# Two value casts moved from GpSimd to VectorE, and batch 2's key-value products, numerators and block 2's first units rearranged, in a fused attention and gated feed-forward kernel

## The chip, the cores and the metric

The kernel runs on one core of one Trainium2 chip. The metric is the device time of one execution in microseconds (us). Five engines work side by side, each through its own queue of instructions in order: TensorE (PE: matrix products, with its weight loads shown as PEld), VectorE (DVE), ScalarE (ACT), GpSimd (POOL) and SyncE (SP, which here only issues transfers). Results of PE land in PSUM, which has eight banks in this kernel's one PSUM tile `ps`; everything else works from the on-chip memory SBUF.

## The reference

Eight batches of linear attention with position weights, followed by a gated feed-forward network over all 4608 tokens:

```python
# q, k, v: (8, 8, 576, 64) float32;  theta = pi/2 * pos / 576
phi(x) = concat(max(x, 0) * cos(theta), max(x, 0) * sin(theta))     # 64 -> 128 features
kv  = einsum('bhsf,bhsd->bhfd', phi(k), v);   z = sum_s phi(k)
num = einsum('bhsf,bhfd->bhsd', phi(q), kv)
den = einsum('bhsf,bhf->bhs', phi(q), z) + 1e-6
x   = (num / den), heads side by side, reshaped to (4608, 512)
out = (gelu(x @ w_gate) * (x @ w_val)) @ w_out                       # 512 -> 1536 -> 512
```

## The kernel before, in words

The attention is worked batch by batch (576 tokens each, eight batches), the feed-forward network block by block (512 tokens each, nine blocks). The code writes out by hand the order in which instructions are given to each engine; no scheduler reorders them. The stages of one batch are these:

- **Loads** (`load`, L77, issued at L80). q, k and v of a batch arrive as float32 in halves of 576 KB. Batch 0 and batches 3 and later are issued from SP's queue, batches 1 and 2 from POOL's queue, which also issues the weights (L94, L95, L98). Each staged tensor has two buffers.
- **Features** (`prep`, L151). Each of nine token groups `j` of q and k is multiplied by its cosine on VectorE (L161) and by its sine on ScalarE (L159), and written as bfloat16 into `qp` or `kp`. There is one `qp` and one `kp` buffer, so the next batch's features wait until the last batch's have been read.
- **The value cast** (`cast_v`, L177, instruction at L178). v is cast from float32 to bfloat16 into `vx`, next to a column of ones that makes the denominators. There are two `vx` buffers, for even and odd batches. Batches 0 and 3 to 7 are cast by VectorE, batches 1 and 2 by GpSimd (L451 and L559), as two instructions of 128x1152 elements a batch.
- **Key-value products** (`kv_unit`, L234). PE does 72 small products (L240) of `kp` and `vx` into banks 6 and 7, head pair by head pair, and ScalarE copies them to `kv_sb` (L249, two instructions).
- **Turning q** (`turn_q`, L190). From batch 2 on, two transposing transfers on SP (L192) turn `qp` into `qT`. Batches 0 and 1 are turned on PE (`turn_j`, L455).
- **Numerators** (`nm_unit`, L279). For each of five tiles of 128 tokens of a batch, PE does eight products of `qT` and `kv_sb` (L281), into two banks (6 and 7 unless `b0` names others), and VectorE makes the quotients (L292 denominator, L293 reciprocal, L294 product) into an `x_sb` tile, of which there are six.
- **Turning x** (`turn_x`, L345). A transposing transfer on SP (L348) puts each `x_sb` tile into its columns of the block's `xT`. For batches 0 and 1 most of this is done on PE (`turn_x_pe`, L352).

A block's feed-forward has twelve `gv_unit`s (L366): eight products of 128x512 (L375, four for the gate, four for the value), a Gelu on ScalarE (L383) and a product on VectorE into `hT` (L384). Units use banks 0 and 1 and banks 2 and 3 in turn, so a unit needs the VectorE product of the unit before the last to be done. A unit can be split into two halves of 256 columns; the first half needs only the first 256 columns of `xT`. The output product (`o_part`, L402, instruction L405) follows one block later, four of twelve accumulation steps after each unit; ScalarE copies the result (L414) and SP stores it (`flush`, L397; L395).

The main loop runs over the blocks n = 1 to 8 and over the units jt = 0 to 11 of each; in block n it also prepares batch b = n + 1. Batch 1 is handled before the loop in the list `order`, which mixes its turning of q, its key-value products, its numerators and the last output products of block 0. In the loop, `t_kv` is the unit after which the key-value products of batch b come, `t_nm` the unit from which its numerators come, one tile a unit; `t_q` and `t_k` place the features of the batch after. Block 1's loop also computes the last features of q(2), has SP turn q(2) after unit 2, and computes k(2)'s features after units 2 to 4 (`prep_third`). Block 2 covers the last 128 tokens of batch 1 and the first 384 of batch 2, so its second 256 columns are numerator tiles 1 and 2 of batch 2. Units 0 and 1 of blocks 1, 2 and 3 are done in halves: first half of unit 0, first half of unit 1, then the second halves.

Of the kernel before, what the change touches and what calls it, by code (L numbers as in the profile page):

```python
# [16 lines left out]
def kernel(  # L17
# [13 lines left out]
    nc = tc.nc  # L31
# [6 lines left out]
    JT = J // 128  # L38
# [3 lines left out]
    NT = 5  # L42
# [21 lines left out]
    def bank(i):  # L64
        return ps[:, i]

    def bank16(i):
        return ps[:, i].bitcast(BF16)
# [69 lines left out]
        for _ in range(n):  # L138
            nc.tensor.matmul(bank(to), lhsT=dummy[:, 0:128], rhs=dummy, start=True, stop=True)  # L139

    act_copy, dve_copy, pool_copy = nc.scalar.copy, nc.vector.tensor_copy, nc.gpsimd.tensor_copy


    phi = {}
# [32 lines left out]
    def cast_v(b, m0, m1, copy, j0=0, j1=R):  # L177
        copy(  # L178
            vx_tiles[b % 2][:, m0:m1, j0:j1, 0:D],
            staged["v", b][:, m0:m1, j0 * D:j1 * D].rearrange("p m (j d) -> p m j d", d=D),  # L180
        )
# [97 lines left out]
    def nm_unit(b, t, b0=6):  # L279
        for h in range(H):  # L280
            nc.tensor.matmul(  # L281
                bank(b0 + h // 4)[:, (h % 4) * (D + 1):(h % 4 + 1) * (D + 1)],
                lhsT=q_cols(b, t, h),
                rhs=kv_sb[b][:, h // 2, h % 2, :],
                start=True,
                stop=True,
            )
        nm = ps[:, b0:b0 + 2, 0:4 * (D + 1)].rearrange("p g (h d) -> p g h d", h=4)
        den = attn2.tile([128, 2, 4], FP32, name="den")
        rec = attn2.tile([128, 2, 4], FP32, name="rec")  # L290
        x = xsp.tile([128, 2, 4, D], BF16, name="x_sb")
        nc.vector.tensor_scalar_add(den, nm[:, :, :, D], EPS)  # L292
        nc.vector.reciprocal(rec, den)  # L293
        nc.vector.tensor_tensor(  # L294
            x,
            nm[:, :, :, 0:D],
            rec[:, :, :, None].to_broadcast([128, 2, 4, D]),
            op=ALU.mult,
        )
        xs[b, t] = x.rearrange("p g h d -> p (g h d)")  # L300
# [44 lines left out]
    def turn_x(b, t):  # L345
        x = xs.pop((b, t))
        for blk, c, o, m in pieces(b, t):
            nc.sync.dma_start_transpose(  # L348
                out=xT_block(blk)[:, :, c:c + m], in_=x[o:o + m, :]
            )  # L350
# [15 lines left out]
    def gv_unit(n, jt, c0=0, w=BLK):  # L366
        xt = xT[n]
        js = slice(jt * 128, (jt + 1) * 128)
        b0 = 2 * (turn[0] % 2)
        turn[0] += 1  # L370
        if n not in hT:
            hT[n] = ffn.tile([128, JT, BLK], BF16, name="hT")
        for g, wt in ((0, wg_sb), (1, wv_sb)):
            for ct in range(CT):
                nc.tensor.matmul(  # L375
                    bank(b0 + g)[:, 0:w],
                    lhsT=wt[:, ct, js],
                    rhs=xt[:, ct, c0:c0 + w],
                    start=(ct == 0),
                    stop=(ct == CT - 1),  # L380
                )
        gel = ffn.tile([128, BLK], FP32, name="gel")
        nc.scalar.activation(gel[:, 0:w], bank(b0)[:, 0:w], AF.Gelu)  # L383
        nc.vector.tensor_mul(  # L384
            hT[n][:, jt, c0:c0 + w], gel[:, 0:w], bank(b0 + 1)[:, 0:w]
        )
# [33 lines left out]
    HALF = BLK // 2  # L420
# [27 lines left out]
        for m in (0, 2):  # L448
            load(nc.gpsimd, name, 2, m, m + 2)
    for m in (0, 2):  # L450
        cast_v(1, m, m + 2, pool_copy)  # L451
    for m in (0, 2):
        load(nc.gpsimd, "v", 2, m, m + 2)

    def turn_j(b, m0, m1, js, to, copy):  # L455

        n = len(js)
        for m in range(m0, m1):
            turn_q_pe(b, m, js, bank16(to)[:, (m - m0) * n * 128:])
        copy(  # L460
            qt_tile(b)[:, :, m0:m1, js[0] * 64:(js[0] + n) * 64].rearrange(
                "f i m (j p) -> f m j i p", j=n
            ),
            bank16(to)[:, 0:(m1 - m0) * n * 128].rearrange(
                "f (m j i p) -> f m j i p", m=m1 - m0, j=n, i=2
            ),
        )
# [68 lines left out]
    for what, *a in order:  # L536
        if what == "o":
            o_part(a[0], range(a[1], a[1] + 4), banks0[a[0]], act_copy)
        if what == "q":
            turn_j(1, a[0], a[1], range(a[2], a[2] + 4), a[3], (dve_copy, act_copy)[a[3] % 2])  # L540
        if what == "q8":
            turn_j(1, 0, 4, (R - 1,), a[0], dve_copy)
        if what == "k":
            prep("k", 1, 0, range(R))
            prep("k", 1, 1, range(7), eng=nc.scalar)
            prep("k", 1, 1, range(7, R))
        if what == "q2":
            prep("q", 2, 1, range(*a), eng=nc.scalar)
            prep("q", 2, 0, range(*a))
        if what == "kv":  # L550
            kv_unit(1)
        if what == "nm":
            nm_unit(1, a[0], a[1])
        if what == "xt":
            turn_x_pe(1, a[0], a[1], act_copy)
    for m in (0, 2):
        load(nc.sync, "q", 3, m, m + 2)
    for m in (0, 2):
        cast_v(2, m, m + 2, pool_copy)  # L559


    def prep_third(name, b, i):
# [4 lines left out]
    def loads(b, names=("q", "k", "v")):  # L567
        for name in names:
            for m in (0, 2):
                load(nc.sync, name, b, m, m + 2)  # L570
# [12 lines left out]
    turn[0] = 1  # L583
    for n in range(1, NB):
        b = n + 1
        t_kv, t_nm, t_q, t_k = {1: (5, 8, 12, 12), 2: (5, 7, 7, 9), 3: (2, 5, 6, 9)}.get(
            n, (1, 2, 4, 8)
        )
        for jt in range(JT):
            if n > 3 or jt > 1:  # L590
                gv_unit(n, jt)
            else:
                for i in range(2):
                    gv_unit(n, i, jt * HALF, HALF)
                    if n == 1:
                        j = JA + 2 * jt + i
                        prep("q", b, 1, (j,), eng=nc.scalar)
                        prep("q", b, 0, (j,))
                        if jt == i == 0:
                            turn_x_pe(1, 3, 5, act_copy)  # L600
            if jt % 3 == 1:
                flush()
            if b < B:
                if n == 1 and jt == 2:
                    prep("q", b, 0, (R - 1,))
                    prep("q", b, 1, (R - 1,), eng=nc.scalar)
                    turn_q(b)
                    nm_unit(1, NT - 1)
                if n == 1 and jt == 3:
                    turn_x(1, NT - 1)  # L610

                late = -(-(BLK - 64 * b) // 128)
                nms = [(b, jt - t_nm)] if 0 <= jt - t_nm < (late if n == 1 else NT) else []
                if n == 2 and jt < 2:
                    nms.append((n, 3 + jt))
                i = jt - t_nm - 1
                if 0 <= i < late:
                    turn_x(b, i)
                    if n == 1 and i == late - 1:
                        loads(b + 1, ("k", "v"))  # L620
                for bt in nms:
                    nm_unit(*bt)
                if jt == t_kv:
                    kv_unit(b)
                i = jt - 2 if n <= 2 else -1
                if 0 <= i < 3:
                    prep_third("k", b, i)
                i = jt - (3 if n == 2 else 0)
                if n in (2, 3) and 0 <= i < 2:
                    cast_v(b, 2 * i, 2 * i + 2, dve_copy)  # L630
                i = jt - 9
                if n > 2 and 0 <= i < 2 and b + 1 < B:
                    cast_v(b + 1, 2 * i, 2 * i + 2, dve_copy)
                if (n, jt) in q3:
                    cosines, sines_ = q3[n, jt]
                    prep("q", 3, 1, sines_, eng=nc.scalar)
                    prep("q", 3, 0, cosines)
                if n > 1 and b + 1 < B:
                    if 0 <= jt - t_q < 3:
                        prep_third("q", b + 1, jt - t_q)  # L640
                    if 0 <= jt - t_k < 3:
                        prep_third("k", b + 1, jt - t_k)
                for c, t in nms:
                    if t == NT - 1:
                        if c + 1 < B:
                            turn_q(c + 1)
                        if c + 2 < B:
                            loads(c + 2)
                        for i in range(-(-(BLK - 64 * c) // 128), NT):
                            turn_x(c, i)  # L650
            if n > 1:
                o_part(
                    4 * (n - 1) + jt // 3,
                    range(4 * (jt % 3), 4 * (jt % 3) + 4),
                    4,
                    act_copy,
                )
# [47 lines left out]
```

## Time and profile before

| What | Value |
|---|---|
| median of 4 runs | 328.16 us |
| the four runs | 327.78, 329.58, 327.08, 328.54 us |
| the profiled execution | 327.78 us, of which the span from first to last instruction is 325.7 us |
| mean granted TensorE clock | 0.997 |
| busy time in the span: PE, DVE, ACT, POOL | 318.4, 167.9, 160.0, 28.3 us |
| L375, full units | 2 x 392 products, 2 x 100.6 us busy |
| L405 | 420 products, 105.8 us busy |
| L178 on DVE | 12 casts, mean 769 ns |
| L178 on POOL | 4 casts, mean 1562 ns |

A product of 512 columns is listed with a mean of 379 ns although the next one begins some 216 ns after it (eight of them take 1.73 us in the chain), since the products run in a pipeline. So "busy" sums can't be added up to the span; distances from start to start can. The profiled execution's time lies 2.1 us above its span.

### The profile page before, as it was taken

Reading aid. Unit: us, or ns where it says so; the run is one execution under the profiler, and the core shown is the slowest. Engines: PE = TensorE matmul, PEld = TensorE weight load, DVE = VectorE, ACT = ScalarE, POOL = GpSimd, SP = SyncE. Lnnn points to the kernel's source line nnn. Section 1 sums busy time; section 2 is a strip of 40 time slices with the busy share of each in tenths; the row PEclk is TensorE's granted clock in tenths of the full one; section 3 lists DMA queues with packets and bytes.
Section 4 is the critical chain, followed back from the end, with each engine's and each line's share of the span. In section 5 each row is a group of like instructions: output and inputs, shape, how many; then the busy total and the mean of one; then the engine's idle time right before and its main releaser. Section 6 shows DMA issues by size and latency. Waiting matters only on the chain.

```text
span 325.7 us, 6332 instructions
## 1 busy us (share of the span) xinstructions
PE 318.4 (98%) x2438; PEld 164.7 (51%) x2438; DVE 167.9 (52%) x406; ACT 160.0 (49%) x341; POOL 28.3 (9%) x43
## 2 busy tenths in 40 slices
PE   8899999999999999999999999999999999999995
PEld 3585556555554564545544545445544444444443
DVE  5863666748765961794485448544532222222211
ACT  8755767946455833574466336642222233222220
POOL 2855462000000000000000000000000000000000
PEclk9999999999999999999999999999999999999998
DMA  7999999982999989959978991764421111111124
GB/s 271 244 192 270 302 345 338 225 132 49 309 140 362 232 104 269 324 104 163 377 160 122 311 295 42 102 104 102 90 65 40 35 32 32 35 32 32 34 65 97
DMA packets 69102, 53.57 MB, mean 164 GB/s; under 512 B 45392, under 2 KB 54352, under 8 KB 69072
## 3 DMA queue, kind: packets, MB, share of 16 engines
q1 hardware_dynamic: 59264, 41.23, 54.5%
q0 software_dynamic: 9648, 11.80, 15.8%
q8 instruction: 19, 0.31, 0.4%
q10 hardware_dynamic: 160, 0.13, 0.1%
q14 instruction: 11, 0.09, 0.1%
HBM read 37.75 MB, written 9.44 MB: 145 GB/s over the span
## 4 chain that ended last, share of the span: by engine, by line
PE 89%; DMA 6%; DVE 1%; POOL 1%; SPq 0%; issue 0%; ACT 0%; DVEq 0%
PE ps L375 54%; PE ps L405 28%; PE ps L281 3%; DMA wv_sb<-in_moe_w_val_dram 2%; PE ps L240 2%; DMA qf<-in_q_dram 2%; DMA qT<-qp 2%; PE ps L666 1%; PE ps L203 1%; POOL wg_sb L94 1%; DVE qp L161 0%; PE ps L356 0%; DVE hT L384 0%; DVE kp L161 0%; SPq L80 0%
## 5 line engine op out<-in xcount | busy, mean ns | idle before, releaser
L384 DVE TENSOR_TENSOR hT<-gel,ps 128x512 bf16<-128x512 f32 (+2 forms) x120 | 75.8, 633 | 132.5 <-PE ps L375 128.6
L383 ACT ACTIVATE gel<-ps 128x512 f32<-128x512 f32 (+2 forms) x120 | 66.7, 556 | 110.1 <-PE ps L375 107.1
L375 PE MATMUL ps<-xT,wv_sb 128*128 128x512 bf16 (+2 forms) x480 | 113.0, 358 | 0.3 <-DMA wv_sb<-in_moe_w_val_dram 0.3
L375 PE MATMUL ps<-xT,wg_sb 128*128 128x512 bf16 (+2 forms) x480 | 112.9, 358 | 0.0
L405 PE MATMUL ps<-wo_sb,hT 128*128 128x512 bf16 x420 | 105.8, 379 | 0.0
L375 PEld LDWEIGHTS <-wv_sb 128*128 128x128 bf16 x480 | 46.3, 98 | 47.7 <-DMA wv_sb<-in_moe_w_val_dram 0.6
L375 PEld LDWEIGHTS <-wg_sb 128*128 128x128 bf16 x480 | 45.8, 98 | 45.8
L405 PEld LDWEIGHTS <-hT 128*128 128x128 bf16 x420 | 38.3, 98 | 39.8
L414 ACT COPY o_sb<-ps 128x512 f32<-128x512 f32 x34 | 19.9, 585 | 29.6 <-PE ps L405 29.6
L159 ACT ACTIVATE qp<-qf,sin_t 128x256 bf16<-128x256 f32 x71 | 31.8, 502 | 1.6 <-DMA qf<-in_q_dram 0.9
L159 ACT ACTIVATE kp<-kf,sin_t 128x256 bf16<-128x256 f32 (+1 forms) x75 | 30.4, 477 | 0.9 <-DMA kf<-in_k_dram 0.9
L294 DVE TENSOR_TENSOR x_sb<-ps,rec 128x512 bf16<-128x512 f32 x38 | 26.3, 692 | 1.5 <-DVE rec L293 0.2
L161 DVE TENSOR_SCALAR qp<-qf,cos_t 128x256 bf16<-128x256 f32 x71 | 21.6, 353 | 4.4 <-DMA qf<-in_q_dram 4.4
L281 PEld LDWEIGHTS <-qT 128*128 128x128 bf16 x304 | 14.6, 98 | 8.2 <-DMA qT<-qp 0.7
L161 DVE TENSOR_SCALAR kp<-kf,cos_t 128x256 bf16<-128x256 f32 x63 | 18.1, 348 | 0.0
L281 PE MATMUL ps<-kv_sb,qT 128*128 128x65 bf16 x304 | 16.1, 194 | 0.4 <-DMA qT<-qp 0.4
L139 PE MATMUL ps<-dummy 128*128 128x512 bf16 x30 | 9.9, 478 | 1.5 <-POOL dummy L113 1.5
L249 ACT CAST kv_sb<-ps 128x260 bf16<-128x260 f32 x14 | 4.6, 382 | 13.0 <-PE ps L240 13.0
L240 PEld LDWEIGHTS <-kp 64*128 64x128 bf16 x504 | 8.6, 95 | 3.1 <-issue 3.0
L178 DVE CAST vx<-vf 128x1152 bf16<-128x1152 f32 x12 | 9.2, 769 | 0.8 <-DMA vf<-in_v_dram 0.8
L240 PE MATMUL ps<-vx,kp 64*128 64x65 bf16 x504 | 9.5, 191 | 0.0
L293 DVE RECIPROCAL rec<-den 128x8 f32<-128x8 f32 x38 | 7.7, 203 | 1.3
(52 smaller groups left out, 91.4 us busy)
## 6 DMA issues: line engine op xcount, KB each, us to landing
out_dram<-o_sb SPq DMA_DIRECT2D x70, 128.0 KB, 2.5
kf<-in_k_dram SPq DMA_DIRECT2D x12, 576.0 KB, 6.5
vf<-in_v_dram SPq DMA_DIRECT2D x12, 576.0 KB, 8.6
qf<-in_q_dram SPq DMA_DIRECT2D x10, 576.0 KB, 5.1
qf<-in_q_dram POOLq DMA_DIRECT2D x4, 576.0 KB, 12.1
kf<-in_k_dram POOLq DMA_DIRECT2D x4, 576.0 KB, 12.8
vf<-in_v_dram POOLq DMA_DIRECT2D x4, 576.0 KB, 10.8
wg_sb<-in_moe_w_gate_dram POOLq DMA_DIRECT2D x6, 256.0 KB, 9.2
```

Of the source, the lines that this page charges most:

```text
L139: nc.tensor.matmul(bank(to), lhsT=dummy[:, 0:128], rhs=dummy, start=True, stop=True)
L159: nc.scalar.activation(o, i, AF.Relu, scale=tab[:, j:j + 1])
L161: (eng or nc.vector).tensor_scalar(o, i, 0.0, tab[:, j:j + 1], op0=ALU.max, op1=ALU.mult)
L178: copy(vx_tiles[b % 2][:, m0:m1, j0:j1, 0:D], staged["v", b][:, m0:m1, j0 * D:j1 * D].rearrange("p m (j d) -> p m j d", d=D),)
L240: nc.tensor.matmul(bank(6 + i)[:, m * (D + 1):(m + 1) * (D + 1)], lhsT=kp[rr, m, j, :], rhs=vx[rr, m, j, :], start=(j == 0), stop=(j == R ...
L281: nc.tensor.matmul(bank(b0 + h // 4)[:, (h % 4) * (D + 1):(h % 4 + 1) * (D + 1)], lhsT=q_cols(b, t, h), rhs=kv_sb[b][:, h // 2, h % 2, :], ...
L294: nc.vector.tensor_tensor(x, nm[:, :, :, 0:D], rec[:, :, :, None].to_broadcast([128, 2, 4, D]), op=ALU.mult,)
L375: nc.tensor.matmul(bank(b0 + g)[:, 0:w], lhsT=wt[:, ct, js], rhs=xt[:, ct, c0:c0 + w], start=(ct == 0), stop=(ct == CT - 1),)
L383: nc.scalar.activation(gel[:, 0:w], bank(b0)[:, 0:w], AF.Gelu)
L384: nc.vector.tensor_mul(hT[n][:, jt, c0:c0 + w], gel[:, 0:w], bank(b0 + 1)[:, 0:w])
L405: nc.tensor.matmul(bank(to), lhsT=hT[n][:, jt, tt * 128:(tt + 1) * 128], rhs=wo_sb[:, jt, :], start=(jt == 0), stop=(jt == JT - 1),)
L414: copy(o_sb, bank(to))
```

## The change

There are four edits. Batches 1 and 2 are no longer cast on GpSimd: v(1) is cast by VectorE after q(1)'s last group has been copied, in the list before the loop, and v(2) by VectorE as one instruction after unit 5 of block 1. In block 1, the key-value products of batch 2 come after unit 7 instead of unit 5, and the numerators of batch 2, with the turning of x, are written at the head of units 9, 10 and 11 instead of at the end of units 8, 9 and 10, into banks 6/7, 4/5 and 6/7. In block 2, units 0 to 3 are done in halves instead of units 0 and 1. And in block 2, k(3)'s features, v(3)'s casts and the key-value products of batch 3 come one unit later.

```diff
-    for m in (0, 2):
-        cast_v(1, m, m + 2, pool_copy)
     for m in (0, 2):
         load(nc.gpsimd, "v", 2, m, m + 2)
...
         if what == "q8":
             turn_j(1, 0, 4, (R - 1,), a[0], dve_copy)
+            for m in (0, 2):
+                cast_v(1, m, m + 2, dve_copy)
...
     for m in (0, 2):
         load(nc.sync, "q", 3, m, m + 2)
-    for m in (0, 2):
-        cast_v(2, m, m + 2, pool_copy)
...
-        t_kv, t_nm, t_q, t_k = {1: (5, 8, 12, 12), 2: (5, 7, 7, 9), 3: (2, 5, 6, 9)}.get(
+        t_kv, t_nm, t_q, t_k = {1: (7, 9, 12, 12), 2: (6, 7, 7, 9), 3: (2, 5, 6, 9)}.get(
             n, (1, 2, 4, 8)
         )
         for jt in range(JT):
-            if n > 3 or jt > 1:
+            if n == 1 and jt >= t_nm:
+                nm_unit(2, jt - t_nm, (6, 4, 6)[jt - t_nm])
+                turn_x(2, jt - t_nm)
+            heads = (0, 2, 4, 2)[n] if n < 4 else 0
+            if jt >= heads:
                 gv_unit(n, jt)
             else:
                 for i in range(2):
-                    gv_unit(n, i, jt * HALF, HALF)
+                    half, unit = divmod(2 * jt + i, heads)
+                    gv_unit(n, unit, half * HALF, HALF)
...
-                late = -(-(BLK - 64 * b) // 128)
-                nms = [(b, jt - t_nm)] if 0 <= jt - t_nm < (late if n == 1 else NT) else []
+                nms = [(b, jt - t_nm)] if n > 1 and 0 <= jt - t_nm < NT else []
                 if n == 2 and jt < 2:
                     nms.append((n, 3 + jt))
+
+                late = -(-(BLK - 64 * b) // 128)
                 i = jt - t_nm - 1
-                if 0 <= i < late:
+                if n > 1 and 0 <= i < late:
                     turn_x(b, i)
-                    if n == 1 and i == late - 1:
-                        loads(b + 1, ("k", "v"))
+                if n == 1 and jt == JT - 1:
+                    loads(3, ("k", "v"))
...
-                i = jt - 2 if n <= 2 else -1
+                i = jt - 1 - n if n <= 2 else -1
                 if 0 <= i < 3:
                     prep_third("k", b, i)
-                i = jt - (3 if n == 2 else 0)
+                i = 2 * (jt - 5) if n == 1 else jt - (4 if n == 2 else 0)
+                if n == 1 and i == 0:
+                    cast_v(b, 0, 4, dve_copy)
                 if n in (2, 3) and 0 <= i < 2:
                     cast_v(b, 2 * i, 2 * i + 2, dve_copy)
```

More of the change, by code (lines that the diff above doesn't have):

```diff
@@ L139, in dummies @@
             nc.tensor.matmul(bank(to), lhsT=dummy[:, 0:128], rhs=dummy, start=True, stop=True)
-    act_copy, dve_copy, pool_copy = nc.scalar.copy, nc.vector.tensor_copy, nc.gpsimd.tensor_copy
+    act_copy, dve_copy = nc.scalar.copy, nc.vector.tensor_copy
     phi = {}
```

## The prediction

> **What bounds the kernel now.** I read the page's busy table first (PE 318.4 us of a 325.7 us span, no other engine above 168), then the chain of waits, then each engine's timeline from 40 to 104 us, where all edits lie.
>
> In the chain, outside the start, one stretch is not PE:
>
> ```profile
> 64.84 1.03 PE L375 MATMUL ps<-xT,wg_sb 128*128 128x512 bf16 x4
> 65.71 1.03 PE L375 MATMUL ps<-xT,wv_sb 128*128 128x512 bf16 x4
> 66.67 1.51 PE L240 MATMUL ps<-vx,kp 64*128 64x65 bf16 x72
> ...
> 67.26 6.53 DMA qT<-qp
> ...
> 73.30 0.19 PE L281 MATMUL ps<-kv_sb,qT 128*128 128x65 bf16 x1
> 73.84 0.40 PE L281 MATMUL ps<-kv_sb,qT 128*128 128x65 bf16 x7 [0.35 <-DMA qT<-qp]
> 74.08 1.02 PE L375 MATMUL ps<-xT,wg_sb 128*128 128x512 bf16 x4
> ...
> 75.80 0.42 PE L281 MATMUL ps<-kv_sb,qT 128*128 128x65 bf16 x8
> 76.06 1.02 PE L375 MATMUL ps<-xT,wg_sb 128*128 128x512 bf16 x4
> 76.92 1.03 PE L375 MATMUL ps<-xT,wv_sb 128*128 128x512 bf16 x4
> 77.86 0.42 PE L281 MATMUL ps<-kv_sb,qT 128*128 128x65 bf16 x8
> ```
>
> (Start and length in us; the line at 67.26 is from the chain, the others from PE's timeline.) The starts matter, since products overlap. The first numerator tile of batch 2 reaches PE at 73.30, does one product and waits for the second transfer that turns q(2), which lands at 67.26 + 6.53 = 73.79. An undisturbed tile takes 0.26 us (75.80 to 76.06), this one 0.78: **0.52 us lost**. Next, four products take 0.86, so the third tile was due at 76.92 + 0.86 = 77.78; it starts at 77.86, just after the second tile's quotients end at 77.80: **0.08 lost**. Last, the key-value products were due at 66.57, begin at 66.67 and take 1.44 us, while the two neighbours take 1.26: **0.28 lost**, of which 0.1 is also seen ahead of the neighbours. Adding one start after another in this way from 40 to 104 us, I find only one other gap above 0.1 us (0.12 at 57.66, not touched). So everything that the edits could free is 0.52 + 0.28 + 0.08 = 0.88 us, 0.27% of the time. That cap governs what follows.
>
> **The change, part by part**, with the order in which both programs give instructions to each engine.
>
> *Numerators.* On PE they don't move. Before, tile 0 follows unit 8; at the head of unit 9 it still follows unit 8, and so for tiles 1 and 2. Ahead of tile 0 stand the same nine units, the key-value products and one tile of batch 1 in both. What sets the wait, the transfers that turn q(2), is gated by q(2)'s last cosine on VectorE (62.01) and SP's queue; SP's order of transfers is unchanged, and nothing ahead of 62 us is moved on VectorE but the cast of v(1) (below). So the landing stays at 73.79 and PE resumes at 74.08: 0. If the key-value products, two units later, run in 1.26, PE comes 0.28 us sooner and waits 0.28 longer: also 0. Banks 4/5 for tile 1 free tile 2 from the quotients just ahead: **−0.08**. On VectorE one cosine of q(3) (0.27 from start to start) now precedes each tile's quotients. Tile 0's cosine waits for the same landing, runs 73.8 to 74.1, and the quotients started at 74.28 anyway. Tiles 1 and 2 come 0.27 later, so `x_sb` of tile 2 is ready at about 80.05 instead of 79.78, and lands 2.4 us later (SP's x transfers there take 2.4 to 2.5), 82.5. Behind them SP issues k(3) and v(3), 0.27 later; k(3)'s first use is a unit later too.
>
> *Block 2's halves.* The second 256 columns were needed at 82.70 with tile 2 landing at 79.8 + 2.4 = 82.2, a margin of 0.5. Now four first halves come first, so they are needed one half-unit pair and one output step later, 2.6 to 2.9 us (82.70 to 85.57 before). The margin becomes some 3 us; as PE did not wait there in this execution, it is worth 0. The cost: four groups of four 256-column products take 1.75 (82.70 to 84.45), a full unit 1.73, so two more split units cost **+0.04** on PE. VectorE gets 2 x 0.42 for 0.69 and ScalarE 2 x 0.39 for 0.60, +0.15 and +0.2 a unit, while a unit with its output step lasts 2.59 on PE and both were idle for 1 to 2 us at these units (1.13 at 86.4 on VectorE, 2.04 on ScalarE).
>
> *v(1) on VectorE.* Two casts, by the DVE row:
>
> ```profile
> 46.66 0.42 DVE L460 COPY qT<-ps 128x512 bf16<-128x512 bf16 x1 [0.69 <-PE ps L203]
> 47.40 1.41 POOL L80 DMA_DIRECT2D vf<-in_v_dram  x2
> 48.28 1.33 PE L240 MATMUL ps<-vx,kp 64*128 64x65 bf16 x72
> ...
> 50.51 0.62 DVE L161 TENSOR_SCALAR qp<-qf,cos_t 128x256 bf16<-128x256 f32 x2 [3.43 <-DMA qf<-in_q_dram]
> ...
> 91.55 0.76 DVE L178 CAST vx<-vf 128x1152 bf16<-128x1152 f32 x1
> ...
> 43.57 3.89 POOL L178 CAST vx<-vf 128x1152 bf16<-128x1152 f32 x2 [2.98 <-DMA vf<-in_v_dram]
> 54.98 1.15 POOL L178 CAST vx<-vf 128x1152 bf16<-128x1152 f32 x1 [6.17 <-DMA vf<-in_v_dram]
> ```
>
> VectorE is free from 47.08 to 50.51, where it waits for q(2). 2 x 0.76 end at 47.84 and 48.60. PE wants the first at 48.28 and the second, half of the 72 products later, at 48.91: margins of 0.44 and 0.31, so 0 on the path; 1.52 of the 3.43 idle is used, and the next VectorE work still waits for q(2). Without that cover the 1.52 us would delay q(2)'s features and batch 1's quotients behind them.
>
> *v(2) on VectorE.* One cast of 128x2304, a shape that the trace doesn't show. Nearest row: 0.76 for half of it, so at most 1.52; the other end is POOL's slowest, 2.8 a half, 5.6. I take 1.5. It follows unit 5's product, which ends at 67.54, where VectorE idled 2.57 us; that idle was the key-value products' and moves, so unit 6's product, due at 68.35, starts at about 69.05, 0.7 late. Its banks are wanted by unit 8 at about 71.4: cover of 1.7 after it. The cast's own reader, the key-value products after unit 7, comes at about 70.0. 0.
>
> *POOL.* v(2)'s two loads no longer stand behind the casts. They are issued when their earlier transfers have landed, near 42 and 43.6 instead of 47.40 and 48.11. The loads of POOL's queue land in order, 1.4 to 1.5 us apart (issue plus landing time: q(2) 48.9 and 50.4, k(2) 51.9 and 53.4, v(2) 54.9 and 56.2), and the transfer engines are full from 30 to 58 us. So v(2) still lands near 55 to 56, and q(2) at 50.4: 0.
>
> The Trainium skill ("SBUF — State Buffer", section "SBUF: two separate sides") speaks against this edit: while VectorE runs certain copies and casts, GpSimd is locked out of a port and can't write the descriptors of its loads. By its example (620 ns become 3100) the two issues, now among VectorE's back-to-back cosines instead of in its idle stretch, would take 5 us more, an estimate; the sum would still not change, since the queue reaches them at 53.4. The rows show 0.70 to 0.75 us for POOL's issues throughout, beside busy VectorE or not. The page also says that a cast on GpSimd blocks VectorE; POOL's first cast did stretch to 2.8 us, but VectorE's cosines beside it kept 0.27 from start to start (nine in 2.44), so freeing VectorE from it is worth nothing by the row.
>
> *Batch 3's key-value products one unit later.* Same work. Numerator tile 0 of batch 3 follows two units later before and one unit later now; between them lie an output step and a unit (2.6 us) for the two copies to `kv_sb` (0.66): 0.
>
> **Sum.** −0.08 + 0.04 = −0.04 us: 327.7 on the profiled execution's own time (327.78). The median of the runs is 0.38 higher, so the same sum on it gives 328.1. I take **328.0**, nearer to the median, since a landing margin of 0.5 becomes 3, which can only help the runs above the profiled one. The runs spread from 327.08 to 329.58, so 0.5% (1.64 us) is about what a measurement of this kernel can tell from no change; the likeliest case's own range is 327.0 to 329.2.
>
> **Rivals.**
>
> *The casts of v(1) come too late (slower).* Place: 48.28 on PE. It begins to decide where one cast takes over 0.92 us (47.08 + 2 x 0.92 = 48.91). At POOL's undisturbed 1.15, 0.47 us is lost; at 2.8, the second ends at 52.68 and 3.77 is lost: 331.8 on the median. To pass 0.5% a cast would have to take 1.74 us. Against it: twelve VectorE casts of this shape have a mean of 0.769. For it: the margin is only 0.31, and all of it hangs on VectorE's in-order queue behind PE's last transposes. 6%.
>
> *v(2)'s early loads take bandwidth from q(2) (slower).* If all of v(2)'s 2 x 576 KB (3.0 us at 1.5 each) went ahead of q(2)'s second half, VectorE would wait until 53.4, and batch 1's first quotients, wanted at 52.66 with 0.5 to spare (their end at 52.16), would stop PE for 2.5: 330.7. It decides from 0.5 us of delay. Against it: in-order landings above. 6%.
>
> *The wait at 73.3 goes after all, or the unprofiled runs hold waits at block 2's start that the halves take away (faster).* All 0.88 less the 0.04 gives 327.3 on the median, still within 0.5%; a gain of 1.64 needs 0.8 us more that this trace doesn't show. The transfers that turn q(2) would have to land 0.5 sooner, for which nothing is moved. 8% beyond 0.5%; smaller gains belong to the no-change case.
>
> *The edit doesn't do what it says:* true of the numerators on PE, and in the sum.
>
> **How the numbers follow.** Forecast and its near neighbours, no change within 0.5%: 80%. Slower 12% (6 + 6), faster 8%. The range goes from 326.7 (all 0.88 gone from the profiled execution's 327.78, and 0.2 for the other runs' waits) to 329.6, which takes in the smaller stalls of both slower rivals (up to 1.4) and leaves their far ends out.
>
> **What will show it.** The first numerator tile of batch 2 still waits for the turned q(2) until about 73.8 to 74; tile 2 starts without a gap; VectorE's two casts lie between 47.1 and 48.7, with key-value products at 48.3; v(2) lands near 55 to 56; the second halves of block 2 begin at about 85.6 without a wait; PE's busy time is the same within 0.3 us. I am wrong if PE shows a new wait on `vx`, on q(2) or on `hT` of unit 6, or if the transfers that turn q(2) land at another time.

## The result, and the profile after

The changed kernel takes 326.83 us in the median of 43 runs (325.98 to 327.96). The kernel before takes 327.70 in 64 runs made beside them (326.50 to 329.78). The ratio of the means is 0.9965, with a 95% interval of 0.9955 to 0.9976: faster by 0.35%, well clear of no change, though inside the 0.5% that the forecast took as its bound.

More telling than the medians is how the runs are spread (counts of runs, rounded to quarters of a microsecond):

```
us       before  changed          us       before  changed
326.00             2              328.00             1
326.25             7              328.25     1
326.50     4       4              328.50     8
326.75     3      14              328.75     8
327.00     6       6              329.00     4
327.25    13       5              329.25     5
327.50     6       3              329.50     3
327.75     2       1              329.75     1
```

The kernel before has two groups of times: 34 runs at or under 328.0 with a mean of 327.14, and 30 above with a mean of 328.88. (It is not the clock: the three profiled executions of the upper group, below, had a mean granted clock of 0.999 to 1.000, and over the 122 runs of the kernel before that were made beside the experiments the mean is 0.9989 in the upper group and 0.9993 in the lower one, 0.04% apart where the times are 0.5% apart.) The changed kernel has no run above 328.0; its mean is 326.81. So of the 1.14 us between the two means (327.957 and 326.815), 30/64 x (328.88 − 327.14) = 0.82 is the upper group going, and 327.14 − 326.81 = 0.33, to rounding, is the rest. The profile of before that the prediction was read from is of the lower group.

The changed kernel's profiled execution (326.73 us, span 324.9) answers to the lines shown of before. These are PE's and VectorE's timelines: start, length, engine, line, operation, shapes and count, and in brackets an idle time before it with what ended it.

```profile
41.73 2.80 DVE L161 TENSOR_SCALAR kp<-kf,cos_t 128x256 bf16<-128x256 f32 x9
...
43.84 1.89 PE L405 MATMUL ps<-wo_sb,hT 128*128 128x512 bf16 x8
45.71 0.38 PE L203 MATMUL ps<-ident,qp 128*128 128x128 bf16 x4
...
46.47 1.42 DVE L178 CAST vx<-vf 128x1152 bf16<-128x1152 f32 x2
47.75 1.33 PE L240 MATMUL ps<-vx,kp 64*128 64x65 bf16 x72
...
66.93 1.36 DVE L178 CAST vx<-vf 128x2304 bf16<-128x2304 f32 x1
68.20 0.68 DVE L384 TENSOR_TENSOR hT<-gel,ps 128x512 bf16<-128x512 f32 x1
...
72.59 0.19 PE L281 MATMUL ps<-kv_sb,qT 128*128 128x65 bf16 x1
73.12 0.40 PE L281 MATMUL ps<-kv_sb,qT 128*128 128x65 bf16 x7 [0.33 <-DMA qT<-qp]
...
75.08 0.42 PE L281 MATMUL ps<-kv_sb,qT 128*128 128x65 bf16 x8
...
77.07 0.42 PE L281 MATMUL ps<-kv_sb,qT 128*128 128x65 bf16 x8
```

VectorE's casts of v(1) end at 47.89, and the key-value products, which need only the first of the two at their start, begin at 47.75 without a wait; the cast of v(2) takes 1.36 and makes unit 6's product start at 68.20, with no one waiting. Tile 0 of batch 2 still waits for the turned q(2), from 72.59 to 73.12. Tile 2 starts at 77.07, when it is due (0.08 gained). From q(1)'s first turning (40.13 before, 39.47 after) to the end of the span it is 285.57 us before and 285.43 after: 0.14 less. What lies ahead of that point is untouched by the edits and simply came 0.66 sooner. (In all 18 profiled executions, of whatever kernel, q(1)'s first turning follows the first value products of block 0's unit 2 by 19.54 to 19.56 us. Those products start anywhere from 19.45 to 21.25; in the profile of before they wait 0.33 us for a weight load.) Inside their spans, then, the two profiled executions show next to nothing of a gain that 107 runs show clearly: most of it is in executions that were not profiled. Outside the spans there is a difference of 0.25 us, 327.78 − 325.7 = 2.08 before and 326.73 − 324.9 = 1.83 after; more on it at the end of the part on why the prediction was right or wrong.

### The profile page after: what moved, and what is told of

It is laid out like the page before. It is cut to its first block, busy times and chain, and to the rows that moved or that the text cites. A ratio compares the mean times of both kernels' runs of the same rounds, so it can differ in the third digit from the quotient of the medians.

```text
span 324.9 us, 6360 instructions
## 1 busy us (share of the span) xinstructions
PE 318.4 (98%) x2454; PEld 166.5 (51%) x2454; DVE 170.4 (52%) x411; ACT 160.0 (49%) x343; POOL 22.1 (7%) x39
## 4 chain that ended last, share of the span: by engine, by line
PE 90%; DMA 5%; ACT 2%; DVE 1%; SPq 1%; issue 0%; DVEq 0%; ACTq 0%
PE ps L375 54%; PE ps L405 28%; PE ps L281 3%; DMA qf<-in_q_dram 3%; PE ps L240 2%; DMA qT<-qp 2%; ACT kp L159 1%; PE ps L671 1%; SPq L80 1%; PE ps L203 1%; PE ps L356 1%; ACT gel L383 0%; DVE qp L161 0%; DVE x_sb L321 0%; SPq L192 0%
## 5 line engine op out<-in xcount | busy, mean ns | idle before, releaser
L375 PEld LDWEIGHTS <-wv_sb 128*128 128x128 bf16 x488 | 47.3, 98 | 46.4
L375 PEld LDWEIGHTS <-wg_sb 128*128 128x128 bf16 x488 | 46.6, 98 | 45.4
L178 DVE CAST vx<-vf 128x1152 bf16<-128x1152 f32 (+1 forms) x15 | 12.0, 806 | 0.8 <-DMA vf<-in_v_dram 0.8
```

Source lines behind the costliest of these rows:

```text
L178: copy(vx_tiles[b % 2][:, m0:m1, j0:j1, 0:D], staged["v", b][:, m0:m1, j0 * D:j1 * D].rearrange("p m (j d) -> p m j d", d=D),)
L375: nc.tensor.matmul(bank(b0 + g)[:, 0:w], lhsT=wt[:, ct, js], rhs=xt[:, ct, c0:c0 + w], start=(ct == 0), stop=(ct == CT - 1),)
```

## The experiments

Each was run beside the kernel before on the same chip (35 runs of it beside the first three sets each, 17 beside the fourth). "Over 328.0" counts the runs above the gap between the two groups.

### First set: one part alone, or one part undone

**e1, the halves alone.** Block 2's first four units in halves, put into the kernel before:

```diff
-            if n > 3 or jt > 1:
+            heads = (0, 2, 4, 2)[n] if n < 4 else 0
+            if jt >= heads:
...
-                    gv_unit(n, i, jt * HALF, HALF)
+                    half, unit = divmod(2 * jt + i, heads)
+                    gv_unit(n, unit, half * HALF, HALF)
```

> The kernel before with block 2's first four units in halves and nothing else. The times of the kernel before lie in two groups, about 326.5 to 327.8 us and 328.2 to 329.8 us (28 of 64 in the upper one); those of the changed kernel lie between 326.0 and 328.0. Theory X (late x): in the upper group the turned x of batch 2's tiles 1 or 2 lands after the second 256 columns of block 2 are due at 82.70, where the profiled execution had 0.45 us to spare, and PE waits some 1.5 us. Then this kernel has no upper group: all times under about 328.0, median 327.0 to 327.3, ratio near 0.997. Theory C (casts): the upper group comes from GpSimd's cast of v(1), which took 2.8 us where others took 1.15, being late for the key-value products. Then the upper group stays, ratio within 0.999 to 1.001. Theory K (batch 3): it comes from k(3) landing late for its features after units 2 to 4 of block 2; then the upper group stays too.

Ratio 1.0006 (0.9981 to 1.0031), 7 of 12 runs over 328.0. The upper group stays; theory X falls.

**e2, the changed kernel without the two additional halved units.**

```diff
-            heads = (0, 2, 4, 2)[n] if n < 4 else 0
+            heads = (0, 2, 2, 2)[n] if n < 4 else 0
```

> The changed kernel with only units 0 and 1 of block 2 in halves, as before; all else changed. Theory X: an upper group of times returns, some 1.5 us above the lower one, in nearly half of the executions; median 327.2 to 328.5, ratio 0.998 to 1.000. Theories C and K: no upper group, median about 326.8 as the changed kernel.

Ratio 0.9970 (0.9954 to 0.9987), 0 of 12 over 328.0, median 326.47. The halves are not needed for the gain.

**e3, the changed kernel with GpSimd's casts.** Both casts are put back to POOL's queue, all else stays changed (the line that defines `pool_copy` is left out here):

```diff
+    for m in (0, 2):
+        cast_v(1, m, m + 2, pool_copy)
     for m in (0, 2):
         load(nc.gpsimd, "v", 2, m, m + 2)
...
-            for m in (0, 2):
-                cast_v(1, m, m + 2, dve_copy)
...
+    for m in (0, 2):
+        cast_v(2, m, m + 2, pool_copy)
...
-                if n == 1 and i == 0:
-                    cast_v(b, 0, 4, dve_copy)
```

> The changed kernel with v(1) and v(2) cast by GpSimd as before, all else changed. Theory C: the upper group returns, ratio 0.998 to 1.000. Theories X and K: as the changed kernel, about 326.8, ratio 0.996 to 0.997; the casts are worth nothing.

Ratio 0.9996 (0.9975 to 1.0018), 3 of 12 over 328.0: the upper group is back, and no gain is left that can be told from none. So the casts make it. But the place that theory C named was wrong: this run's profile fell in the upper group (328.89 us), and GpSimd's casts were quick there:

```profile
42.02 4.28 DVE L161 TENSOR_SCALAR kp<-kf,cos_t 128x256 bf16<-128x256 f32 x9
46.22 0.81 DVE L161 TENSOR_SCALAR kp<-kf,sin_t 128x256 bf16<-128x256 f32 x2
46.96 0.68 DVE L460 COPY qT<-ps 128x1024 bf16<-128x1024 bf16 x1
...
42.67 1.22 POOL L178 CAST vx<-vf 128x1152 bf16<-128x1152 f32 x1 [2.97 <-DMA vf<-in_v_dram]
44.13 1.18 POOL L178 CAST vx<-vf 128x1152 bf16<-128x1152 f32 x1 [0.23 <-DMA vf<-in_v_dram]
...
44.13 1.89 PE L405 MATMUL ps<-wo_sb,hT 128*128 128x512 bf16 x8
47.69 0.38 PE L203 MATMUL ps<-ident,qp 128*128 128x128 bf16 x4 [1.67 <-DVE qT L460]
```

The same rows in the profile of before:

```profile
42.39 2.44 DVE L161 TENSOR_SCALAR kp<-kf,cos_t 128x256 bf16<-128x256 f32 x9
45.28 0.69 DVE L460 COPY qT<-ps 128x1024 bf16<-128x1024 bf16 x1
...
44.51 1.89 PE L405 MATMUL ps<-wo_sb,hT 128*128 128x512 bf16 x8
46.23 0.39 PE L203 MATMUL ps<-ident,qp 128*128 128x128 bf16 x4
```

In e3 the casts took 1.2 us each, and VectorE's nine cosines beside them 4.28 instead of 2.44. Behind the cosines in VectorE's queue stands the copy that empties bank 2, and PE turns q(1)'s last group in that bank: it was due at 44.13 + 1.73 = 45.86 and began at 47.69. That gave theory P (port): GpSimd and VectorE block each other, now one and now the other; if VectorE loses, PE loses 1.8 us.

**e4, block 1's rearrangement alone**, with GpSimd's casts and the old block 2:

```diff
-        t_kv, t_nm, t_q, t_k = {1: (5, 8, 12, 12), 2: (5, 7, 7, 9), 3: (2, 5, 6, 9)}.get(
+        t_kv, t_nm, t_q, t_k = {1: (7, 9, 12, 12), 2: (5, 7, 7, 9), 3: (2, 5, 6, 9)}.get(
...
+            if n == 1 and jt >= t_nm:
+                nm_unit(2, jt - t_nm, (6, 4, 6)[jt - t_nm])
+                turn_x(2, jt - t_nm)
...
```

> The kernel before with block 1's rearrangement alone: batch 2's key-value products after unit 7, its numerators written at the head of units 9 to 11, banks 4/5 for tile 1. Theory X: two groups of times as before, both about 0.1 us lower by the banks; ratio 0.999 to 1.000. If the numerators' place matters after all (x earlier by more than the 0.08 us), the upper group shrinks or goes. Theory C and K: two groups, too.

Ratio 1.0000 (0.9977 to 1.0022), 3 of 12 over 328.0: two groups, nothing gained that can be measured. The 0.08 of the banks is too small for it.

### Second set: which cast, and by which way

**f1, only v(1) to VectorE** (the two lines of e3 for v(1), the other way round, in the kernel before).

> The kernel before with only v(1)'s two casts moved to VectorE (v(2) stays on GpSimd). Theory P (port): in the upper group of times GpSimd's casts of v(1) get ahead of VectorE's nine cosines of k(1), which then take 4.28 us instead of 2.44, the copy of turned q behind them comes 1.7 us late, and PE waits for its bank before q(1)'s last group. Then this edit alone removes the upper group: all times under 328.0, ratio 0.995 to 0.998, cosines 2.4 to 2.8 us in the trace. Rival R: the upper group needs both casts or comes from v(2)'s: then two groups stay, ratio 0.999 to 1.001.

Ratio 0.9978 (0.9958 to 0.9998), 0 of 12 over 328.0, median 326.78, cosines 2.58 in the profile. This one edit takes the upper group away.

**f2, only v(2) to VectorE**, ahead of the key-value products where they stood before:

```diff
-    for m in (0, 2):
-        cast_v(2, m, m + 2, pool_copy)
...
+                if n == 1 and jt == 4:
+                    cast_v(b, 0, 4, dve_copy)
```

> The kernel before with only v(2)'s cast moved to VectorE, as one instruction after unit 4 of block 1, ahead of the key-value products after unit 5 (v(1) stays on GpSimd). Theory P: two groups of times as in the kernel before, ratio 0.999 to 1.002. Rival R: no upper group, ratio 0.995 to 0.998.

Ratio 1.0048 (1.0019 to 1.0076). Two groups stay, 8 runs from 327.6 to 328.6 and 4 from 330.5 to 331.1, as theory P says, but 1.3 and 1.9 us higher than the two groups of before beside it, which neither theory expected. PE's timeline shows why:

```profile
64.58 1.03 PE L375 MATMUL ps<-xT,wv_sb 128*128 128x512 bf16 x4
67.15 1.34 PE L240 MATMUL ps<-vx,kp 64*128 64x65 bf16 x72 [1.54 <-DVE vx L178]
```

VectorE reaches the cast only after k(2)'s last cosines, and the key-value products after unit 5 wait for it. This is the work that the changed kernel's other move covers: with the cast on VectorE, the products must come later, and after unit 7 they do not wait.

**f3, one number:** q(1)'s last group turned in bank 6, both casts left on GpSimd.

```diff
-        + [("q8", 2), ("o", 1, 4), ("o", 2, 4), ("kv",), ("q2", 0, 2), ("o", 3, 4)]
+        + [("q8", 6), ("o", 1, 4), ("o", 2, 4), ("kv",), ("q2", 0, 2), ("o", 3, 4)]
```

> The kernel before with one number changed: q(1)'s last group is turned in bank 6 instead of bank 2, so PE doesn't wait for VectorE's copy of bank 2 ahead of it; both casts stay on GpSimd. Theory P: VectorE's cosines are stretched as often as before, but PE has no wait there beyond some 0.2 to 0.4 us at the key-value products: the upper group of times goes or shrinks to under 328.2, ratio 0.996 to 0.999. If the loss runs by another way (features of k(1) late, or GpSimd's loads of v(2) late), two groups stay, ratio 0.999 to 1.001.

Ratio 0.9977 (0.9957 to 0.9996), 0 of 12 over 328.0, highest 327.52. PE no longer needs the copy of bank 2 at that point, and the upper group is gone with the casts where they were. The edit acts first at PE's turning in bank 6, at 45.94 in this run's profile, when the first cast has begun (42.99) and the cosines have ended (44.54), so it is not how they meet that it changes. So the loss runs by that bank; that it runs by no other way is what the times say, since no trace caught stretched cosines with bank 6 (h3, below).

**f4, the numerators really one unit later** on PE, in the changed kernel:

```diff
-        t_kv, t_nm, t_q, t_k = {1: (7, 9, 12, 12), 2: (6, 7, 7, 9), 3: (2, 5, 6, 9)}.get(
+        t_kv, t_nm, t_q, t_k = {1: (7, 10, 12, 12), 2: (6, 7, 7, 9), 3: (2, 5, 6, 9)}.get(
...
                 if n == 1 and jt == JT - 1:
+                    nm_unit(2, 2, 6)
+                    turn_x(2, 2)
                     loads(3, ("k", "v"))
```

> The changed kernel with batch 2's numerators really one unit later on PE: tile 0 behind unit 9, tile 1 behind unit 10, tile 2 behind unit 11 of block 1. Both traces have PE wait 0.5 us at tile 0 for the turned q(2), landing near 73.1 to 73.8. If that wait is the next thing to go, PE reaches tile 0 at about 74.3, after the landing, and the time falls by 0.5 us against the changed kernel, to about 326.3, ratio 0.994 to 0.996. If x for block 2 then comes late (tile 0 is due at about 78.6 and would land at about 78.2), PE waits there instead and the time stays at 326.8, ratio 0.996 to 0.997.

Ratio 1.0031 (1.0011 to 1.0051), a loss that neither line expected. Timelines of ScalarE, VectorE, SP and PE:

```profile
75.04 0.91 ACT L159 ACTIVATE qp<-qf,sin_t 128x256 bf16<-128x256 f32 x2 [1.71 <-DMA qT<-qp]
75.13 0.42 PE L281 MATMUL ps<-kv_sb,qT 128*128 128x65 bf16 x8
...
76.46 0.69 DVE L384 TENSOR_TENSOR hT<-gel,ps 128x512 bf16<-128x512 f32 x1 [1.05 <-ACT gel L383]
...
77.33 0.16 DVE L292 TENSOR_SCALAR den<-ps 128x8 f32<-128x8 f32 x1
...
78.48 3.08 SPq L348 DMA_TRANSPOSE xT<-x_sb  x2
...
79.09 0.42 PE L281 MATMUL ps<-kv_sb,qT 128*128 128x65 bf16 x8
81.03 0.60 PE L375 MATMUL ps<-xT,wg_sb 128*128 128x256 bf16 x4 [1.51 <-DMA xT<-x_sb]
```

PE's wait for the turned q is gone (no bracket at 75.13), but ScalarE now waits 1.71 us for the same landing with q(3)'s sines, ahead of unit 9's Gelu; VectorE waits for that Gelu, and tile 0's quotients stand behind it: PE had finished tile 0 at about 75.4, its quotients begin at 77.33, its x is turned from 78.48, and block 2, due at 79.35, starts at 81.03. The 0.5 us wait was exchanged for one of 1.7 (79.35 to 81.03).

### Third set: the changed kernel again, and what is left at bank 2

**g1** is the changed kernel again, **g2** f1's and f3's edits together, **g3** the changed kernel with q(1)'s last group in bank 6, and **g4** the kernel before against itself. The edits are those shown.

> The changed kernel once more, beside the next three on one chip. Theory P: one group of times, median 326.4 to 326.9, ratio 0.995 to 0.998; in the trace PE waits 0.1 to 0.2 us at q(1)'s last group, since GpSimd's two issues of v(2)'s loads still take 0.3 us from VectorE's cosines (2.7 to 2.8 us for the nine).

Ratio 0.9971 (0.9949 to 0.9992), median 326.58, 0 of 12 over 328.0. The small wait was not there this time, since the collision went the other way. In POOL's and VectorE's timelines of g1

```profile
41.27 0.70 POOL L80 DMA_DIRECT2D vf<-in_v_dram  x1 [1.70 <-DMA wo_sb<-in_moe_w_out_dram]
42.76 2.51 POOL L80 DMA_DIRECT2D vf<-in_v_dram  x1 [0.79 <-DMA vf<-in_v_dram]
...
42.16 2.44 DVE L161 TENSOR_SCALAR kp<-kf,cos_t 128x256 bf16<-128x256 f32 x9
46.42 0.42 DVE L458 COPY qT<-ps 128x512 bf16<-128x512 bf16 x1 [0.69 <-PE ps L203]
```

the cosines are undisturbed, and the issue of v(2)'s second load takes 2.51 us where others take 0.72. In the first profile of the changed kernel the issues took 0.70 and 0.72 and the cosines 2.80.

> The kernel before with v(1) cast by VectorE and q(1)'s last group turned in bank 6; nothing else. If both edits only guard against the same loss, this is as either alone, ratio 0.996 to 0.998, one group of times. If the casts on VectorE, now behind the copy of bank 6, come late for the key-value products, 0.2 to 0.5 us are lost, ratio 0.997 to 0.999.

Ratio 0.9971 (0.9947 to 0.9994), 0 of 12 over 328.0: as either edit alone, so the two guard against the same loss.

> The changed kernel with q(1)'s last group turned in bank 6. Theory P: the 0.1 to 0.2 us that PE still waits there go: median 0.1 to 0.2 us under the changed kernel's, ratio 0.994 to 0.998. If nothing is left there: as the changed kernel.

Ratio 0.9961 (0.9941 to 0.9981), median 326.54 against g1's 326.58: the lowest ratio of all, but not to be told from the changed kernel.

> The kernel before once more, against itself. Two groups of times, ratio 1.000 within its interval. Where the profiled execution is of the upper group (about 4 in 10), theory P expects VectorE's nine cosines of k(1) at 4.0 us or more instead of 2.44, GpSimd's two casts of v(1) at about 2.4 us in sum instead of 3.9, and a wait of PE of 1.5 to 1.8 us for the copy of turned q ahead of q(1)'s last group; in the lower group none of these.

Ratio 0.9989 (0.9965 to 1.0013), 4 of 12 over 328.0. The profile was of the lower group: cosines 2.44, GpSimd's two casts 3.91 in sum, q(1)'s last group at 46.13 as due.

### Fourth set: the kernel before in its upper group

**h1 and h2** are one profiled execution each of the kernel before, **h3** is one of f3's kernel; **h4** casts v(1) on GpSimd in four instructions:

```diff
-    for m in (0, 2):
-        cast_v(1, m, m + 2, pool_copy)
+    for m in range(4):
+        cast_v(1, m, m + 1, pool_copy)
```

> The kernel before, one look. If the time is over 328.2: nine cosines of k(1) at 4.0 us or more, GpSimd's two casts of v(1) at about 2.4 us in sum, PE waits 1.5 to 1.8 us ahead of q(1)'s last group. If under 327.8: cosines 2.44, casts about 3.9 in sum, no wait. Anything else speaks against theory P.

> As the look before: one of the two pictures, and the one that its time calls for.

Both took 329.13 us, and both show the picture foretold. VectorE's, GpSimd's and PE's timelines of h1:

```profile
42.31 4.29 DVE L161 TENSOR_SCALAR kp<-kf,cos_t 128x256 bf16<-128x256 f32 x9
46.52 0.81 DVE L161 TENSOR_SCALAR kp<-kf,sin_t 128x256 bf16<-128x256 f32 x2
47.25 0.67 DVE L460 COPY qT<-ps 128x1024 bf16<-128x1024 bf16 x1
...
43.22 1.23 POOL L178 CAST vx<-vf 128x1152 bf16<-128x1152 f32 x1 [2.96 <-DMA vf<-in_v_dram]
44.66 1.20 POOL L178 CAST vx<-vf 128x1152 bf16<-128x1152 f32 x1 [0.21 <-DMA vf<-in_v_dram]
...
44.42 1.89 PE L405 MATMUL ps<-wo_sb,hT 128*128 128x512 bf16 x8
47.98 0.38 PE L203 MATMUL ps<-ident,qp 128*128 128x128 bf16 x4 [1.67 <-DVE qT L460]
```

and the same rows of g4, the lower group of the same code:

```profile
42.29 2.44 DVE L161 TENSOR_SCALAR kp<-kf,cos_t 128x256 bf16<-128x256 f32 x9
44.66 0.61 DVE L161 TENSOR_SCALAR kp<-kf,sin_t 128x256 bf16<-128x256 f32 x2
45.18 0.68 DVE L460 COPY qT<-ps 128x1024 bf16<-128x1024 bf16 x1
...
43.45 3.91 POOL L178 CAST vx<-vf 128x1152 bf16<-128x1152 f32 x2 [2.97 <-DMA vf<-in_v_dram]
...
44.40 1.89 PE L405 MATMUL ps<-wo_sb,hT 128*128 128x512 bf16 x8
46.13 0.39 PE L203 MATMUL ps<-ident,qp 128*128 128x128 bf16 x4
```

Read the pair down the columns: cosines 4.29 against 2.44, the copy of bank 2 at 47.25 against 45.18, q(1)'s last group 3.56 us behind the products ahead of it against 1.73. GpSimd's casts are the mirror image, 2.4 us in sum against 3.9. Nor is the loss shared out over the nine cosines: in h1 two of them take 1.24 and 1.23 us, one beside each cast, where the median of the nine is 0.35. In the lower group it is the first cast alone that is held: 2.82 us of the 3.91 in g4, and the second takes 1.15.

> The kernel before with q(1)'s last group in bank 6, one look. Theory P: where the nine cosines take 4 us or more, PE still has no wait over 0.4 us between 43 and 52 us, and the time is under 327.9.

The cosines took 2.44 here, so the case that was looked for did not come up. The time was 328.28, above the 327.9 that was named for that case: PE waited for a weight load near the start (the first value products of block 0's unit 2 begin at 21.25 instead of 20.57 in the profile of before) and reached q(1) at 40.80 instead of 40.13. That wait is in none of the edits; it makes part of the spread inside each group. That bank 6 covers the stretch rests on f3's times alone; no trace shows the stretch and the cover together.

> The kernel before with v(1) cast by GpSimd in four instructions of 128x576 instead of two of 128x1152. Theory P: GpSimd gets in between VectorE's instructions at more places, each time for half as long (0.6 us instead of 1.15): fewer executions without any loss, more in between; mean not below that of the kernel before, ratio 0.999 to 1.004. If the casts on GpSimd were harmless as such, ratio 0.999 to 1.001 with the same two groups.

Ratio 0.9998 (0.9972 to 1.0024), 7 of 12 over 328.0, four of these between 328.0 and 328.4, where the kernel before has 4 of 64. That fits shorter and more frequent collisions, but the mean doesn't move, so this run alone decides nothing.

## Why the prediction was right or wrong

The time, 326.83, lies in the range (326.7 to 329.6) and within 0.5% of before, as the likeliest case had it. The forecast of no gain beyond −0.04 us was wrong: the gain is 0.35%, at a place where the prediction had written 0. That the time lies in the range is luck: the range's lower end was worked out from PE's gaps in one execution, of which the largest, the wait for the turned q(2), is still there, and not from the loss that went. Of the 1.17 us by which 328.0 was too high, 0.46 is its base: the median of the four runs was 328.16, that of all 64 is 327.70.

- **The step that failed** is the last sentence on GpSimd: "VectorE's cosines beside it kept 0.27 from start to start (nine in 2.44), so freeing VectorE from it is worth nothing by the row." The row was true of the one profiled execution, in which GpSimd lost: its first cast took 2.8 us instead of 1.15. A cast stretched to more than twice its length is the sign of a fight, and who wins it was taken as fixed. The runs showed that VectorE can lose instead: its cosines then take 4.29, and 1.8 us are lost on PE (e3, h1 and h2, all the upper-group executions that were profiled; 30 of 64 runs lie in that group). Worth: 0.82 of the 1.14 us between the means.
- **The rule that the prediction weighed.** The Trainium skill ("SBUF — State Buffer", section "SBUF: two separate sides") calls the pair of ports that GpSimd shares with VectorE an exclusive lock: whichever starts first, a GpSimd instruction or a VectorE instruction in a two-port mode, has the pair for its whole instruction, and the other blocks. The runs agree in both directions (cosines 2.44 or 4.29; casts 3.9 or 2.4 in sum), and so do the two cosines held for the length of a cast in h1; no trace shows the ports or the mode of the cosines themselves. That rule speaks of one instruction; in g4 the first cast comes 1.67 us late (2.82 less 1.15), the length of several cosines. The prediction weighed that rule against one row and let the row win. Which side wins in an execution stays open. The first cast starts when v(1) has landed, 0.65 to 0.91 us after the first cosine in the three upper-group profiles and 0.89 to 1.18 after it in the eight others that have the casts on GpSimd, so its moment alone does not decide.
- **The cap** "everything that the edits could free is 0.52 + 0.28 + 0.08 = 0.88 us" counted PE's gaps of one execution, which held none of this loss. It also hid how little cover there was: the copy of bank 2 ended at 45.28 + 0.69 = 45.97 in that profile, and PE wanted the bank at 46.23, 0.26 later (the lines of before are shown with e3). That margin was there to read; in the upper group the copy starts 2.07 later (47.25 against 45.18), which leaves the 1.8 lost.
- **The spread of the runs** was read as noise. Four runs were shown, two at 327.1 to 327.8 and two at 328.5 to 329.6. The third rival did say that unprofiled runs may hold waits, but put them at block 2's start and at the turned q; e1 and e2 showed that the halves there are worth nothing that can be measured.
- **Numerators:** right. They do not move on PE, the wait for the turned q(2) stays (0.5 us before and after), tile 2 gains 0.08. f4 showed in addition that moving them for real loses 0.3%.
- **Casts on VectorE hidden:** right. v(1)'s pair took 1.42 (predicted 1.52), v(2)'s 1.36 (1.5), and neither made PE wait. What the later key-value products are for was taken as given; f2 put the price of leaving them at 1.54 us.
- **GpSimd's loads of v(2):** right on the landing, which stays near 55 to 56 (41.48 + 13.1 and 42.94 + 13.1), and wrong that POOL's issues take 0.70 to 0.75 us throughout. In the profile of before itself the six issues at L94 have a mean of 0.87, the longest 1.26, and beside the cosines one issue took 2.51 (g1). Where both issues took their 0.70 and 0.72, as in the first profile of the changed kernel, the nine cosines took 2.80, 0.36 more, and PE came 0.14 late to q(1)'s last group (45.57 due, 45.71).
- **The slower rivals** did not occur: no wait on the cast of v(1), and q(2)'s first cosine at 50.17 against 50.51.
- **The other 0.33 us**, between the lower group and the changed kernel, lies for the most part outside the span from first to last instruction. The prediction took the 2.1 us by which the time exceeds the span as fixed. It is 1.79 in the mean of the changed kernel's runs (1.73 to 1.83) and 2.04 in the 122 runs of the kernel before beside the experiments: 0.25 less. It goes with v(1)'s casts: the other runs that have them on VectorE (e2, f1, f4, g1, g2, g3) have means of 1.77 to 1.82, and those that have them on GpSimd (e1, e3, e4, f2, f3, g4, h4) 1.99 to 2.19. With f1's one edit it is 1.82 against 2.04 beside it, which covers the 0.18 by which f1's mean (326.82) lies under the lower group there (327.00). Spans alone hardly differ: 325.03 in the mean of the changed kernel, 324.94 to 325.09 in the lower groups of the four sets. What these 0.25 us are made of stays open, since no trace shows anything outside the span.

## What to carry to other kernels

Before a profile's rows are summed, look at how the runs are spread: two groups can mean, as here, that some race is decided differently from execution to execution, and one profile shows one side of it only. Where GpSimd works beside a row of VectorE instructions, an instruction of either that is listed at twice its usual length tells of the race, and its price is the other side's delay, followed to the next bank or buffer that someone waits for. The cure can be on either side: take the work off GpSimd (f1), or give the waiting engine a bank that isn't in the queue behind it (f3), each worth 0.2% here.

## What the hardware showed unexpectedly

The same instructions in the same order met in two ways (by the two groups of times, in the slower way in 30 of 64 runs, and in 47 of the 122 beside the experiments): GpSimd's two casts of 128x1152 in 2.4 us and VectorE's nine cosines in 4.29, or 3.9 and 2.44. What one wins the other loses, 1.5 us of casts or 1.9 of cosines. The issue of a load by GpSimd, usually 0.72 us, took 2.51 once beside the same cosines. VectorE got casts of 1.42 and 1.36 us more to do (busy 170.4 us instead of 167.9) and the kernel became faster, since the engine that had helped it was also the one that held it up. The time outside the span went from 2.04 to 1.79 us with v(1)'s casts off GpSimd.
